# An mLSTM cell feeding a GELU feed-forward: the second chunk's cell moved into the first up projection, the first down projection with rows of w_out outermost, the first M spread by TensorE

## The chip, the cores and the metric

The kernel runs on one core of one Trainium2 chip. The metric is the device time of one execution in microseconds. The engines are named as in the profile: PE is TensorE's matmul, PEld its weight load, DVE is VectorE, ACT is ScalarE, POOL is GpSimd, SP is SyncE, whose queue issues nearly all transfers.

## The reference

An mLSTM cell over 4 batches, 8 heads, 768 steps and head size 40, then a feed-forward with exact GELU over the 3072 tokens that come out (320 values each, hidden size 2048):

```python
for t in range(S):
    m_new = np.maximum(f_gate[:, :, t] + m, i_gate[:, :, t])
    f_stab = np.exp(f_gate[:, :, t] + m - m_new)
    i_stab = np.exp(i_gate[:, :, t] - m_new)
    C = f_stab * C + i_stab * einsum('bhd,bhe->bhde', vt, kt)
    n = f_stab * n + i_stab * kt
    h_tilde = einsum('bhde,bhe->bhd', C, qt)
    denom = np.maximum(np.abs(einsum('bhd,bhd->bh', n, qt)), 1.0)
    y[:, :, t] = sigmoid(o_gate[:, :, t]) * h_tilde / denom
x = y.transpose(0, 2, 1, 3).reshape(B * S, H * D)
h = x @ w_in
out = (0.5 * h * (1.0 + erf(h / sqrt(2)))) @ w_out
```

The two weights come in as 64-bit floats; everything else is 32-bit.

## The kernel before, in words

**Chunks.** The 768 steps are cut into six chunks of 128. A chunk holds 4 batches of 128 tokens, 512 tokens in all. For each chunk a *cell* makes x (transposed, tile xT), an *up projection* makes g = gelu(x w_in) in eight steps, and a *down projection* makes the output from g and w_out. The order of a chunk is: up projection, then its down projection with the next chunk's cell woven in.

**The cell, per batch b (block n = 4c + b).** `turn` transposes k and q on PE and copies them out on ACT. The weights W[n] of the attention-like scores are exp(a_s - M_t), masked to s <= t: M, a running maximum per step, has to stand on all 128 partitions. Before, M is stored to a DRAM tile M_d and loaded back spread over the partitions (tile Mb, 512 KB a block, `load_M`); POOL masks it (`affine_select`), ACT takes the exps (L272, eight instructions with a bias of their own; for blocks 1 to 3 DVE subtracts first, L268, and one exp does, L269). `scores` multiplies q and k on PE (ps) and multiplies W into it on DVE (L317); it also forms the state update pc and the far part from the state (pf), with POOL scaling the values (vw) and the state. `values` multiplies W with v (ph), adds the far part (hs), and then gates and divides on POOL and DVE into a tile y. `turn_y` transposes y (px), and DVE and ACT copy the halves into xT.

**The weights.** w_in comes in 10 pieces and w_out in 16 (piece f is 128 rows of w_out). `fetch` loads raw bits into one of four buffers; `convert(i)` starts piece i and finishes piece i - 1: five DVE instructions and two ACT relus between them. The finish frees a buffer and issues fetch(i + 4). The first four up steps need pieces 0 to 4, the others 5 to 9.

**The up and down projections.** An up step takes two PSUM banks of the four-bank ring "mm" (which also holds the scores' banks and the down accumulators), 20 matmul records and two gelus on ACT. A down part is four rows of w_out for one batch; the four parts of batch 0 come first, so the first output needs all 16 rows. The accumulator goes out through o_sb.

**What sets the order.** Nothing is scheduled by the compiler: each engine works through its instructions in the program's order, and waits are semaphores between engines. SP's queue is in order too: a transfer that waits for a buffer holds those issued after it. `run_first` is the first cell with conversions 0 to 5; the rest of the conversions stand between the first up steps and inside the first four down parts; `run(fill)` is each later cell with 16 down parts placed in it by hand. The lookahead for q, k, v and o is six blocks (NLD); Mb has four buffers.

Of the kernel before, what the change touches and what calls it, by code (L numbers as in the profile page):

```python
# [16 lines left out]
I23 = 2.0 ** 23  # L17


@with_exitstack  # L20
def kernel(
# [72 lines left out]
    M_d = dram.tile([NCH, BH, L], F32, name="M_d")  # L94

    def load(n):

        if n >= NCH * B:
            return
        c, b = divmod(n, B)  # L100
        for src, dst in ((q, qb), (k, kb), (v, vb), (o_gate, ob)):
            nc.sync.dma_start(out=dst[n % NLD][:, :, 0:D],
                              in_=src[b, :, c * L:(c + 1) * L, :].rearrange("h p d -> p h d"))
# [3 lines left out]
    def load_M(n, eng=nc.sync):  # L107
# [5 lines left out]
        eng.dma_start(out=Mb[n].rearrange("p h l -> p (h l)"),  # L113
                      in_=M_d[c, b * H:(b + 1) * H, :].rearrange("h l -> (h l)").unsqueeze(0).to_broadcast([P, H * L]))
# [34 lines left out]
    for c0, c1 in ((0, 1), (1, NCH)):  # L149
# [92 lines left out]


    fetch(0)
    load(1)
    fetch(1)
    load(2)
    fetch(2)
    load(3)
    fetch(3)  # L250
    nc.sync.dma_start(out=M_d[1:NCH].rearrange("c p l -> p c l"), in_=M[:, 1:NCH])
# [7 lines left out]
    def weights_of(n):  # L259

        c, b = divmod(n, B)
        W[n] = wts.tile([P, H, L], F32, name="W", tag="W")
        M_n = Mb.pop(n)
        nc.gpsimd.affine_select(out=M_n, in_=M_n, compare_op=OP.is_ge, fill=1.0e30, base=0,  # L264
                                pattern=[[0, H], [1, L]], channel_multiplier=-1)
        if 0 < n < B:

            nc.vector.tensor_tensor(out=M_n, in0=M_n, in1=per_head(aT, c, b).to_broadcast([P, H, L]), op=OP.subtract)  # L268
            nc.scalar.activation(out=W[n], in_=M_n, func=AF.Exp, scale=-1.0)  # L269
        else:  # L270
            for h in range(H):
                nc.scalar.activation(out=W[n][:, h, :], in_=M_n[:, h, :], func=AF.Exp, scale=-1.0,  # L272
                                     bias=aT[:, c, b * H + h:b * H + h + 1])
        if c > 0:
            load_M(n + NM)

    def output_gate(n):
        nc.scalar.activation(out=ob[n % NLD], in_=ob[n % NLD], func=AF.Sigmoid)  # L278

    class Cell:  # L280


        def __init__(self, c):
            self.c = c
            self.qT, self.kT, self.far, self.ys = {}, {}, {}, {}
# [11 lines left out]
        def weighted(self, n):  # L297
            c, b = divmod(n, B)
            vw = two.tile([P, H, D1], F32, name="vw", tag="vw")
            nc.gpsimd.tensor_tensor(out=vw, in0=vb[n % NLD], in1=per_head(ewT, c, b).to_broadcast([P, H, D1]),  # L300
                                    op=OP.mult)
            return vw

        def scores(self, b, between=None):
            c, n = self.c, self.c * B + b
            kT, qT = self.kT.pop(b), self.qT.pop(b)
            if c + 1 < NCH and between is None:
                vw = self.weighted(n)
# [9 lines left out]
            if between is not None:  # L318
                between()
                vw = self.weighted(n)  # L320
# [3 lines left out]
            if c + 1 < NCH:  # L324
                for p in range(NP):
                    for hip in range(2):
                        nc.tensor.matmul(pc[halves[hip], p, :], kb[n % NLD][:, 2 * p + hip, :], vw[:, 2 * p + hip, :],  # L327
                                         start=True, stop=True)
# [19 lines left out]
        def values(self, b):  # L348
            c, n = self.c, self.c * B + b
# [5 lines left out]
            hs = two.tile([P, H, D1], F32, name="hs", tag="hs")  # L355
            if c > 0:
                nc.vector.tensor_tensor(out=hs, in0=ph, in1=self.far.pop(b), op=OP.add)
            else:
                nc.scalar.copy(out=hs, in_=ph)

            ys = self.ys[b] = two.tile([P, DM + R], F32, name="y", tag="y")
            y = ys[:, 0:DM].rearrange("p (h d) -> p h d", d=D)
            nc.gpsimd.tensor_tensor(out=y, in0=hs[:, :, 0:D], in1=ob[n % NLD], op=OP.mult)  # L363
# [7 lines left out]
            if c > 0:  # L371
                load(n + NLD)

        def turn_y(self, b):

            ys, t = self.ys.pop(b), slice(b * L, (b + 1) * L)
            for k0, n in ((0, 3), (3, 2)):
                px = ps_tr.tile([P, n, L], F32, name="px", tag="tr")
                for k in range(n):
                    nc.tensor.transpose(px[:, k, :], ys[:, (k0 + k) * R:(k0 + k + 2) * R], ident)  # L380
                nc.vector.tensor_copy(out=xT[0:R, k0:k0 + n, t], in_=px[0:R])  # L381
                nc.scalar.copy(out=xT[R:P, k0:k0 + n, t], in_=px[R:P])  # L382

        def run_first(self):

            self.turn(0), weights_of(0), convert(0)
            self.scores(0, decays)
            for b in range(1, B):
                weights_of(b)
            for b in range(B):  # L390
                if b > 0:
                    self.turn(b), convert(b)
                    if b == B - 1:
                        load(B)
                    self.scores(b), self.turn_y(b - 1)
                output_gate(b), self.values(b)
            load(B + 1)
            self.turn_y(B - 1), convert(B), convert(B + 1)

        def run(self, fill):  # L400

            n = self.c * B
            self.turn(0), weights_of(n), fill(2)
            self.turn(1), weights_of(n + 1), weights_of(n + 2), fill(1)
            self.scores(0), fill(1)
            self.turn(2), weights_of(n + 3)
            for b in range(B):
                output_gate(n + b)
            fill(1)
            self.scores(1), self.values(0), fill(2)  # L410
            self.turn(3), fill(1)
            self.scores(2), self.values(1), fill(1)
            self.turn_y(0), fill(1)
            self.scores(3), self.values(2), fill(1)
            self.turn_y(1), fill(1)
            self.values(3), fill(1)
            self.turn_y(2), fill(2)
            self.turn_y(3), fill(1)
# [18 lines left out]
    def down_steps(c, g):  # L437
        hold = {}

        def part(b, f0, f1):  # L440
# [5 lines left out]
            if f1 == NF:  # L446
                o_sb = outp.tile([P, DM], F32, name="o_sb", tag="o_sb")
                nc.scalar.copy(out=o_sb, in_=po)  # L448
                nc.sync.dma_start(out=out[b * S + c * L:b * S + (c + 1) * L, :], in_=o_sb)

        return [lambda b=b, f=f: part(b, f, f + 4) for b in range(B) for f in range(0, NF, 4)]

    def feeder(steps):
        todo = list(steps)

        def fill(n):
            for _ in range(min(n, len(todo))):
                todo.pop(0)()
        return fill

    Cell(0).run_first()
    gate_ctx.close()
    gp = ctx.enter_context(tc.tile_pool(name="gp", bufs=1))
    done = [n_in // 2 + 1]

    def conv(n):
        for _ in range(n):
            if done[0] <= len(pieces):  # L470
                convert(done[0])
                done[0] += 1

    for c in range(NCH):
        g = gp.tile([P, NF, TG], F32, name="g", tag="g")
        ups, downs = up_steps(g), down_steps(c, g)
        if c == 0:

            conv(1)
            for j, step in enumerate(ups):  # L480
                step()
                conv(1 if j == 2 else 2)
                if j in (2, 5):
                    load(B + 2 + j // 3)
                if j >= NF // 2 - B:
                    load_M(B + j - (NF // 2 - B))
            for i in range(1, 4):
                at, old = n_in + 4 * (i + 1), downs[i]
                downs[i] = lambda at=at, old=old: (conv(at + 1 - done[0]), old())
            downs[4] = lambda old=downs[4]: (load(2 * B), load(2 * B + 1), old())  # L490
        else:
            for step in ups:
                step()
        fill = feeder(downs)
        if c + 1 < NCH:
            Cell(c + 1).run(fill)
        fill(B * NF)
# [30 lines left out]
```

## Time and profile before

| | |
|---|---|
| median of 3 runs | 597.93 us (597.92 to 598.04) |
| the profiled execution | 598.42 us, span 596.6 us |
| PE busy | 552.7 us (93% of the span) |
| DVE, ACT, POOL busy | 205.2, 227.1, 81.1 us |
| mean granted TensorE clock | 0.977 |
| moved by DMA | 43.62 MB |

The page gives busy time by engine, the span in 40 slices, the DMA queues, the chain that ended last, and groups of instructions by line. A row of the timeline has start, duration, engine, line, operation, tiles, count, and in brackets the idle time before it with what ended it. A row of the windows has the stretch, its length, busy time of PE, PEld, DVE, ACT and POOL with their instruction counts, the granted clock, the share of DMA, and GB/s. A matmul on 32-bit floats shows as two records.

### The profile page before, as it was taken

The numbers are of one execution on the slowest core, as the hardware profiler recorded it, in microseconds if no ns is written. First come the engines' busy times: TensorE is split into PE (matmuls) and PEld (weight loads), VectorE is DVE, ScalarE is ACT, GpSimd is POOL, SyncE is SP. The second block draws the span as 40 slices with busy tenths as digits, with TensorE's granted clock in tenths as the row PEclk, the third lists the DMA queues.
The fourth block names the chain that finished last, engine by engine and source line by source line (L and its number), as shares of the span: only waits on it lengthen the run. The fifth ranks groups of instructions, "written<-read, shape, count | busy, mean of one in ns | idle before, by whom it ended". The sixth has DMA issues, their size and how long they took to land.

```text
span 596.6 us, 9412 instructions
## 1 busy us (share of the span) xinstructions
PE 552.7 (93%) x3850; PEld 355.7 (60%) x3850; DVE 205.2 (34%) x447; ACT 227.1 (38%) x496; POOL 81.1 (14%) x130
## 2 busy tenths in 40 slices
PE   2585999469999999999999999999999999999997
PEld 2474555347754577754577754577754577744575
DVE  6487888545610025610025600035600033500000
ACT  2654666752122382122481132481132581132100
POOL 3321000303210013310022300022400000100000
PEclk9998899769999999999999999999999999999999
DMA  9977878629820036510046600036000000000000
GB/s 193 203 125 118 164 162 217 226 73 162 137 36 1 0 121 123 88 33 1 1 138 115 96 17 0 1 150 104 13 12 0 1 12 12 12 12 0 1 22 22
DMA packets 111017, 43.62 MB, mean 73 GB/s; under 512 B 101248, under 2 KB 104512, under 8 KB 110976
## 3 DMA queue, kind: packets, MB, share of 16 engines
q1 hardware_dynamic: 110352, 40.92, 33.8%
q10 hardware_dynamic: 624, 2.11, 1.0%
q8 instruction: 30, 0.49, 0.4%
q14 instruction: 11, 0.09, 0.0%
HBM read 38.99 MB, written 4.03 MB: 72 GB/s over the span
## 4 chain that ended last, share of the span: by engine, by line
PE 79%; DVE 10%; issue 4%; DMA 4%; POOL 2%; ACT 1%; SPq 0%; DVEq 0%; POOLq 0%; ACTq 0%
PE po L445 34%; PE pu L430 29%; PE ps L314 3%; PE ph L354 3%; PE pt L292 3%; PE px L380 2%; PE pf L332 2%; DVE sig L232 2%; DMA bits<-in_moe_w_out_dram 2%; PE pf L327 1%; DVE pow L237 1%; DVE pow L225 1%; DMA bits<-in_moe_w_in_dram 1%; DMA Mb<-M_d 1%; DVE sig L230 1%
## 5 line engine op out<-in xcount | busy, mean ns | idle before, releaser
L445 PE MATMUL po<-w_out,g 128*128 128x320 f32 x768 | 224.3, 441 | 7.3 <-DVE w_out L239 7.3
L430 PE MATMUL pu<-xT,w_in 64*128 64x512 f32 x960 | 212.0, 597 | 0.4 <-DVE xT L381 0.2
L445 PEld LDWEIGHTS po<-w_out,g 128*128 128x128 f32 x768 | 142.0, 192 | 62.2 <-DVE w_out L239 9.9
L430 PEld LDWEIGHTS pu<-xT,w_in 64*128 64x128 f32 x960 | 97.8, 189 | 112.1 <-issue 109.2
L317 DVE TENSOR_TENSOR W<-ps,W 128x512 f32<-128x512 f32 x48 | 30.9, 685 | 256.4 <-PE ps L314 251.1
L433 ACT ACTIVATE g<-pu 128x512 f32<-128x512 f32 x96 | 52.0, 593 | 125.8 <-PE pu L430 125.8
L382 ACT COPY xT<-px 64x384 f32<-64x384 f32 (+1 forms) x48 | 17.9, 420 | 115.6 <-DVE xT L381 115.6
L272 ACT ACTIVATE W<-Mb,aT 128x128 f32<-128x128 f32 x168 | 50.8, 392 | 2.6 <-POOL Mb L264 2.5
L345 POOL TENSOR_TENSOR state<-state,dec 64x164 f32<-64x164 f32 x32 | 14.8, 461 | 232.6 <-PE pf L332 231.4
L314 PE MATMUL ps<-qT,kT 64*128 64x128 f32 x384 | 30.6, 304 | 8.2 <-ACT qT L295 8.2
L363 POOL TENSOR_TENSOR y<-hs,ob 128x320 f32<-128x320 f32 x24 | 19.4, 807 | 137.1 <-ACT ob L278 57.5
L314 PEld LDWEIGHTS ps<-qT,kT 64*128 64x128 f32 x384 | 25.7, 204 | 18.4 <-ACT qT L295 9.6
L264 POOL TENSOR_SCALAR_AFFINE_SELECT Mb<-Mb 128x1024 f32<-128x1024 f32 x24 | 28.1, 1192 | 60.3 <-DMA Mb<-M_d 60.0
L448 ACT COPY o_sb<-po 128x320 f32<-128x320 f32 x24 | 10.2, 426 | 58.3 <-PE po L445 42.8
L354 PE MATMUL ph<-vb,W 128*64 128x41 f32 x768 | 28.4, 235 | 2.6 <-DVE W L317 2.6
L354 PEld LDWEIGHTS ph<-vb,W 128*64 128x64 f32 x768 | 26.3, 145 | 5.9 <-DVE W L317 3.7
L381 DVE COPY xT<-px 64x384 f32<-64x384 f32 (+1 forms) x48 | 21.0, 475 | 16.7 <-PE px L380 16.4
L227 ACT ACTIVATE pow<-pow,e_hi 128x320 f32<-128x320 uint32 (+1 forms) x26 | 16.2, 622 | 23.9 <-DVE pow L225 23.8
L292 PE MATMUL pt<-ident,kb 128*128 128x128 f32 x96 | 17.3, 309 | 6.0 <-ACT kT L295 6.0
L295 ACT COPY kT<-pt 128x512 f32<-128x512 f32 x24 | 14.0, 585 | 23.0 <-PE pt L292 22.9
L380 PE MATMUL px<-ident,y 128*128 128x128 f32 x120 | 18.7, 291 | 3.0 <-DVE y L369 3.0
L292 PEld LDWEIGHTS pt<-ident,kb 128*128 128x128 f32 x96 | 12.8, 157 | 13.8 <-ACT kT L295 6.5
(74 smaller groups left out, 360.2 us busy)
## 6 DMA issues: line engine op xcount, KB each, us to landing
Mb<-M_d SPq DMA_DIRECT2D x20, 512.0 KB, 4.1
bits<-in_moe_w_in_dram SPq DMA_DIRECT2D x20, 256.0 KB, 5.0
bits<-in_moe_w_out_dram SPq DMA_DIRECT2D x16, 320.0 KB, 3.2
qb<-in_q_dram SPq DMA_DIRECT2D x24, 160.0 KB, 4.7
kb<-in_k_dram SPq DMA_DIRECT2D x24, 160.0 KB, 4.8
vb<-in_v_dram SPq DMA_DIRECT2D x24, 160.0 KB, 5.0
ob<-in_o_gate_dram SPq DMA_DIRECT2D x24, 160.0 KB, 4.3
out_dram<-o_sb SPq DMA_DIRECT2D x24, 160.0 KB, 1.8
```

What stands on the lines that cost most here:

```text
L264: nc.gpsimd.affine_select(out=M_n, in_=M_n, compare_op=OP.is_ge, fill=1.0e30, base=0, pattern=[[0, H], [1, L]], channel_multiplier=-1)
L272: nc.scalar.activation(out=W[n][:, h, :], in_=M_n[:, h, :], func=AF.Exp, scale=-1.0, bias=aT[:, c, b * H + h:b * H + h + 1])
L292: nc.tensor.transpose(pt[:, p, :], src[n % NLD][:, 2 * p:2 * p + 2, :].rearrange("p h d -> p (h d)"), ident)
L314: nc.tensor.matmul(ps[hip][:, p, :], kT[r, p, :], qT[r, p, :], start=True, stop=True)
L317: nc.vector.tensor_tensor(out=w, in0=ps[hip], in1=w, op=OP.mult)
L354: nc.tensor.matmul(ph[r, h, :], Pm[:, h, r], vb[n % NLD][:, h, :], start=True, stop=True)
L363: nc.gpsimd.tensor_tensor(out=y, in0=hs[:, :, 0:D], in1=ob[n % NLD], op=OP.mult)
L380: nc.tensor.transpose(px[:, k, :], ys[:, (k0 + k) * R:(k0 + k + 2) * R], ident)
L381: nc.vector.tensor_copy(out=xT[0:R, k0:k0 + n, t], in_=px[0:R])
L430: nc.tensor.matmul(pu[e], w_in[r, blk, i * P:(i + 1) * P], xT[r, (blk - e) % NK, :], start=(blk == 0), stop=(blk == NK - 1))
L433: nc.scalar.activation(out=g[:, f + e * (WP // P), :], in_=pu[e], func=AF.Gelu)
L445: nc.tensor.matmul(po, g[:, f, b * L:(b + 1) * L], w_out[:, f, :], start=(f == 0), stop=(f == NF - 1))
```

## The change

Four things are edited together.

1. The order of the steps is written as text. Each word is one step: T turn, M mask, W weights, S scores, C carry (the state part of the old `scores`), V values, Y finish (gate and divide), X turn_y, G gate, U an up step, F a down part or row, K a conversion, P a first fetch, L a load of a block's q, k, v, o, B a load of Mb, D decays, R the store of M; the digit is the block.
2. The second chunk's cell stands in the first up projection (UP_0) and runs over into the first down (DOWN_0).
3. The first down takes row f of w_out for all four batches at once, in four accumulators.
4. For chunk 0, M is spread over the partitions by PE: a column of the identity, repeated, as stationary operand, times M. ACT reads the result in PSUM, and the mask is laid on W after the exp. M_d and Mb are left for the later chunks.

Besides, y is written in place into the o tile, now 384 wide, so a block's load for six blocks on stands behind X in place of V; and px of chunk 0 takes the ring mm.

```diff
+FIRST = """
+    W0 T0 P W1 W2 D L1 P K M0 P P T1 S0 V0 M1 L2 R C0 K S1 G0 V1 M2 K G1 T2 Y0 K G2 X0 W3 L3 K S2 L4 C1 B4 V2 Y1 X1
+    T3 G3 M3 Y2 B5 S3 L5 C2 B7 V3 K C3 Y3 B6 X2 X3"""
+UP_0 = """
+    M0 T0 K G0 U L6 W0 S0 M1 C0 W1 M2 T1 M3 U K K U S1 V0 W2 L8 C1 U K W3 T2 K U K L7 Y0 K U U K K U T3 G1 V1 L9 S2
+    G2 S3 K C2 V2 K Y1 F F Y2 X0 F K F F K K X1 F K C3"""
+DOWN_0 = """
+    V3 K F K F X2 F F F F G3 K K K F F Y3 K F X3 F"""
+DOWN = """
+    M0 T0 W0 F F M1 M2 T1 W1 W2 F S0 C0 F M3 T2 W3 G0 G1 G2 G3 F S1 C1 V0 Y0 F F T3 F S2 C2 V1 Y1 F
+    X0 F S3 C3 V2 Y2 F X1 F V3 Y3 F X2 F F X3 F"""
...
-    ob = [const.tile([P, H, D], F32, name=f"ob{n}") for n in range(NLD)]
+    ob = [const.tile([P, DM + R], F32, name=f"ob{n}") for n in range(NLD)]
...
-        if c0 == 0:
-            nc.scalar.dma_start(out=M_d[0], in_=M[:, 0])
-            for n in range(B):
-                load_M(n, nc.scalar)
...
+        def mask(self, b):
+            t, fill = (Mb[self.c * B + b], 1.0e30) if self.c > 0 else (W[b], 0.0)
+            nc.gpsimd.affine_select(out=t, in_=t, compare_op=OP.is_ge, fill=fill, base=0,
+                                    pattern=[[0, H], [1, L]], channel_multiplier=-1)
+
+        def weights(self, b):
+            n = self.c * B + b
+            W[n] = wts.tile([P, H, L], F32, name="W", tag="W")
+            if self.c > 0:
+                M_n = Mb.pop(n)
+            for h in range(H):
+                r = b * H + h
+                if self.c > 0:
+                    src = M_n[:, h, :]
+                else:
+                    if h % 4 == 0:
+                        pm = ps_mm.tile([P, 4, L], F32, name="pm", tag="mm")
+                        for j in range(4):
+                            nc.tensor.matmul(pm[:, j, :], ident[0:BH, r + j:r + j + 1].to_broadcast([BH, P]), M[:, 0, :],
+                                             start=True, stop=True)
+                    src = pm[:, h % 4, :]
+                nc.scalar.activation(out=W[n][:, h, :], in_=src, func=AF.Exp, scale=-1.0, bias=aT[:, self.c, r:r + 1])
+            if self.c > 0:
+                load_M(n + NM)
...
+        def row(f):
+            if f == 0:
+                hold["po"] = [ps_mm.tile([P, DM], F32, name="po", tag="mm") for b in range(B)]
+            for b in range(B):
+                nc.tensor.matmul(hold["po"][b], g[:, f, b * L:(b + 1) * L], w_out[:, f, :],
+                                 start=(f == 0), stop=(f == NF - 1))
+                if f == NF - 1:
+                    send(b, hold["po"][b])
...
+    for c in range(-1, NCH):
         if c == 0:
...
+        steps = dict(K=conv, P=first_fetch, L=load, R=store_M, B=load_M, D=decays)
         if c + 1 < NCH:
+            cell = Cell(c + 1)
+            steps |= dict(M=cell.mask, W=cell.weights, G=cell.gate, T=cell.turn, S=cell.scores, C=cell.carry,
+                          V=cell.values, Y=cell.finish, X=cell.turn_y)
+        if c >= 0:
+            g = gp.tile([P, NF, TG], F32, name="g", tag="g")
+            steps |= dict(U=in_turn(up_steps(g)), F=in_turn(down_steps(c, g)))
+            play(UP_0 if c == 0 else "U " * (NF // 2), **steps)
+        play(FIRST if c < 0 else "F " * (B * NF // 4) if c + 1 == NCH else DOWN_0 if c == 0 else DOWN, **steps)
```

More of the change, by code (lines that the diff above doesn't have):

```diff
@@ L295, in turn, with scores @@
                 nc.scalar.copy(out=store[b], in_=pt)
[L297 to L308, printed above, removed]
+        def scores(self, b):
+            n = self.c * B + b
+            kT, qT = self.kT.pop(b), self.qT[b]
             ps = [ps_mm.tile([P, NP, L], F32, name="ps", tag="mm") for hip in range(2)]
@@ L324, in scores @@
             if c + 1 < NCH:
+                vw = two.tile([P, H, D1], F32, name="vw", tag="vw")
+                nc.gpsimd.tensor_tensor(out=vw, in0=vb[n % NLD], in1=per_head(ewT, c, b).to_broadcast([P, H, D1]),
+                                        op=OP.mult)
                 for p in range(NP):
@@ L384, in run_first @@
[L384 to L398, printed above, removed]
@@ L454, in feeder, with in_turn @@
+    def in_turn(steps):
         todo = list(steps)
[L456 to L476, printed above, removed]
-        if c == 0:
[L479 to L494, printed above, removed]
-        if c + 1 < NCH:
-            Cell(c + 1).run(fill)
-        fill(B * NF)
```

128 lines of the change are left out of this document (56 added, 72 removed).

## The prediction

> **What bounds the kernel now.** I read the page first, then busy time by stage, then the stretches in which PE idles.
>
> ```profile
> span 596.6 us, 9412 instructions
> PE 552.7 (93%) x3850; PEld 355.7 (60%) x3850; DVE 205.2 (34%) x447; ACT 227.1 (38%) x496; POOL 81.1 (14%) x130
> ```
>
> PE is the bound over the whole span; the question is where its other 44 us lie. Windows at the stage borders (first column the stretch, then its length, busy time and instructions of each engine, granted clock, DMA share, GB/s):
>
> ```profile
> 0.00:58.70 58.70, 31.73 (x326) 26.52 (x326) 39.78 (x83) 27.56 (x54) 16.20 (x42) 0.97 0.86 159
> 58.70:97.70 39.00, 38.82 (x160) 20.79 (x160) 34.06 (x74) 26.66 (x46) 1.34 (x1) 0.92 0.83 178
> 97.70:170.80 73.10, 59.80 (x501) 43.92 (x500) 41.83 (x92) 31.30 (x75) 17.39 (x23) 0.88 0.73 146
> 170.80:205.30 34.50, 34.50 (x161) 15.41 (x160) 0.00 (x0) 9.31 (x16) 0.00 (x0) 1.00 0.02 5
> 205.30:259.50 54.20, 54.20 (x502) 41.28 (x500) 23.44 (x52) 23.07 (x59) 14.19 (x20) 1.00 0.48 98
> 160.00:596.00 436.00, 433.15 (x2938) 272.35 (x2936) 94.80 (x210) 143.51 (x327) 51.03 (x69) 1.00 0.18 40
> ```
>
> In order: cell of chunk 0; first up projection; first down projection with cell 1 inside; then the same two stages one chunk later, undisturbed. From 160 us on PE is busy 433.15 of 436 us, so nothing is to be won there. The first up takes 39.0 against 34.5 us, the first down 73.1 against 54.2, for the same instructions: 4.5 + 18.9 = 23.4 us are lost. The first cell's 58.7 us is a latency chain with PE half idle. These 82 us hold everything the edit can move. PE in the first down (start, duration, in brackets the idle before it and its releaser):
>
> ```profile
> 109.17 1.12 PE L292 MATMUL pt<-ident,kb 128*128 128x128 f32 x4 [6.03 <-ACT kT L295]
> 121.27 1.43 PE L445 MATMUL po<-w_out,g 128*128 128x320 f32 x2 [4.72 <-DVE w_out L239]
> 123.32 1.44 PE L445 MATMUL po<-w_out,g 128*128 128x320 f32 x2 [0.62 <-DVE w_out L239]
> 126.69 2.50 PE L445 MATMUL po<-w_out,g 128*128 128x320 f32 x4 [1.93 <-DVE w_out L239]
> 140.24 0.60 PE L292 MATMUL pt<-ident,kb 128*128 128x128 f32 x4
> ```
>
> 6.03 + 4.72 + 0.62 + 1.93 = 13.3 us of plain idling. Behind each idle the clock is low: the same four transposes take 1.12 us at 109 and 0.60 at 140, which with slow matmuls makes up the other 5.6 us. The chain and SP's own timeline say why:
>
> ```profile
> 102.49 6.65 DMA Mb<-M_d
> 119.48 5.04 DMA bits<-in_moe_w_out_dram
> 109.03 10.37 SPq L113 DMA_DIRECT2D Mb<-M_d  x4
> ```
>
> A token block needs all 16 rows of w_out before its sum is complete, so the first block waits for the whole conversion, and the last raw rows ("bits") sit in SP's queue behind four Mb loads that wait for buffers for 10.37 us.
>
> **The change, part by part.** *Rows of w_out outermost in the first down.* The count of matmuls stays (16 rows x 4 blocks); row f is needed only when it is used, so a late row delays 2.2 us of work instead of a block. Alone it costs nothing: four accumulators take the four banks of the mm ring, which no score or up step needs by then; the four output copies fall together at the end, but the next up step needs only the first two banks.
>
> *Cell 1 inside the first up.* PE's work until the second up projection is that of the undisturbed pair, 34.5 + 54.2 = 88.7 us, less the first turn (0.9) that fits in the wait for the last xT copy: 87.8. DVE must fit in: one conversion of a w_in piece and one of a w_out piece, each a window around exactly one:
>
> ```profile
> 59.00:61.75 2.75, 2.75 (x7) 1.58 (x9) 2.65 (x6) 1.90 (x4) 0.00 (x0) 0.50 1.46 143
> 92.18:94.23 2.05, 2.05 (x13) 1.13 (x12) 1.95 (x6) 1.48 (x3) 0.00 (x0) 1.00 0.80 245
> ```
>
> After the first cell 21 K steps stay: 4 x 2.75 + one mixed 2.4 + 16 x 2.05 = 46.2, less 1.0 as the last only finishes; with cell 1's 23.44 DVE has 68.7 us of work under 87.8 of PE. DVE is no bound.
>
> ACT is tighter. In the up stretch before the last gelu (order text UP_0 up to the eighth U):
>
> ```profile
> 143.36 1.16 PE L314 MATMUL ps<-qT,kT 64*128 64x128 f32 x16
> 144.45 0.67 PE L327 MATMUL pf<-vw,kb 128*64 128x41 f32 x16
> 144.94 0.77 PE L332 MATMUL pf<-state,qT 128*64 128x82 f32 x16
> 145.54 1.08 PE L354 MATMUL ph<-vb,W 128*64 128x41 f32 x32
> L227 ACT ACTIVATE pow<-pow,e_hi 128x320 f32<-128x320 uint32 (+1 forms) x26 | 16.2, 622 | 23.9 <-DVE pow L225 23.8
> L295 ACT COPY kT<-pt 128x512 f32<-128x512 f32 x24 | 14.0, 585 | 23.0 <-PE pt L292 22.9
> L433 ACT ACTIVATE g<-pu 128x512 f32<-128x512 f32 x96 | 52.0, 593 | 125.8 <-PE pu L430 125.8
> 110.92 2.45 ACT L272 ACTIVATE W<-Mb,aT 128x128 f32<-128x128 f32 x8
> L272 ACT ACT_TABLE_LOAD x5 | 6.4, 1283 | 0.1
> 109.63:113.37 3.74, 3.74 (x14) 2.91 (x13) 2.80 (x4) 3.73 (x10) 1.60 (x2) 0.55 0.64 225
> ```
>
> Eight pairs of gelu at about 1.06 = 8.5; four blocks of eight exps at 2.45 = 9.8; the relus of nine K steps, two each at 0.62 = 11.2; six copies of turns at 0.585 = 3.5; a gate 0.5; and seven table loads at 1.28 = 9.0, since exp and gelu now alternate (gelu, exp, gelu, exp, gelu, exp, gelu; sigmoid is still loaded for the first gate). Sum 42.5. PE in that stretch: 34.5 + two more turns 1.8 (each two sets of four transposes at 0.60, less their overlap) + two scores 2.3 + two carries 2.6 (0.67 + 0.77, less overlap) + one values 1.0 = 42.2. So ACT is level with PE, and what decides is when each gelu frees its banks. Walking the order with these durations, from the first U at 0: gelu 1 ends at 5.4; the exps of blocks 0 and 1 at 11.5; gelu 2 at 15; gelu 3 at 19, when PE is just ready for U4; gelu 4 at 25. Before gelu 5 stand relus, a table load and the exps of block 3, copies, relus and another load: it ends at 34.9, while PE wants its banks for U7 at 33.1. One stall, **1.8 us**; bounds 0 (the copies run ahead) and 8 x 3.74 = 29.9 (a load and eight exps ahead of every gelu).
>
> That window (a table load and eight exps, 3.74 us, ACT busy 3.73) also bears on a rule. The Trainium skill, page "ScalarE: Activation LUTs", section "What ACT_TABLE_LOAD costs", puts a switch at 1283 ns plus a drain of about 1380 ns, and its section "Table sets: the hidden batching unit" says to do all calls of one set before switching, which speaks against this order. The load agrees with the row; a drain doesn't show in it. By that page the seven switches would cost 7 x 1.38 = 9.7 us more, and the time would be 586.7.
>
> *Clock at the start of the up.* The first cell still leaves PE sparse, so the first up starts slow again: 39.0 x (1 - 0.92) = **3.1 us**. Bounds 0 (PE dense from the new matmuls) and 4.5 (the whole loss of that stage).
>
> *Bits for the last rows.* Four buffers, so a fetch goes out when the piece four earlier is done. The last one goes out at the second K of DOWN_0, some 76 us after the first U; a landing takes 3.2 us (median) to 5.04, with a load of q, k, v and o beside it, and its K is due 4 to 5 us later: **1.0 us**, bounds 0 and 5.04.
>
> ```profile
> bits<-in_moe_w_out_dram SPq DMA_DIRECT2D x16, 320.0 KB, 3.2
> 0.00:125.00 125.00, 86.25 (x578) 57.84 (x578) 92.02 (x195) 72.81 (x145) 23.45 (x50) 0.91 0.82 175
> Mb<-M_d ACTq DMA_DIRECT2D x4, 512.0 KB, 8.1
> ```
>
> By volume it holds: 125 us at 175 GB/s is 21.9 MB; the four 512 KB Mb loads of chunk 0 go (-2.1), two blocks of loads (+1.3) and one Mb (+0.5) move ahead of the last bits: 21.6 MB, 123 us, with the last piece due near 140. The Mb loads still hold SP until exps are done, but each set of exps is done by 31 us after the first U, and the bits queued behind have 4 to 14 us to spare.
>
> *First M by TensorE, and the first cell's order.* This removes the M_d store, the four loads, the subtractions on DVE and one-instruction exps; it adds 32 matmuls (32 rows, 128 columns) and cuts three one-instruction blocks of exps into eight each, on ACT, which isn't the chain there.
>
> ```profile
> 7.43 1.11 PE L292 MATMUL pt<-ident,kb 128*128 128x128 f32 x4
> 11.74 1.11 PE L292 MATMUL pt<-ident,qb 128*128 128x128 f32 x4 [3.20 <-DVE aT L177]
> 13.76 2.08 PE L314 MATMUL ps<-qT,kT 64*128 64x128 f32 x16 [0.90 <-ACT qT L295]
> 21.20 0.33 DVE L188 COPY dec<-pd 128x160 f32<-128x160 f32 x1 [1.05 <-PE pd L186]
> 21.81 5.25 DVE L268 TENSOR_TENSOR Mb<-Mb,aT 128x1024 f32<-128x1024 f32 x3 [0.29 <-POOL Mb L264]
> 30.42 0.17 DVE L365 SCALAR_TENSOR_TENSOR den<-hs 128x8 f32<-128x8 f32 x1 [3.36 <-ACT hs L359]
> 40.79:49.13 8.34, 6.63 (x16) 1.00 0.24 66
> 47.09 0.17 DVE L365 SCALAR_TENSOR_TENSOR den<-hs 128x8 f32<-128x8 f32 x1 [1.43 <-ACT hs L359]
> 58.73 2.07 PE L430 MATMUL pu<-xT,w_in 64*128 64x512 f32 x3 [0.22 <-DVE xT L381]
> ```
>
> A matmul of f32 shows as two records. One block of M is 16: between 2.08 (the scores, two row halves at once) and 16 x 1.11/4 = 4.4 (turns). I take 3.3, between them as the shape is a turn's and the count a score's. Two blocks and the decays follow the first turn, which ends at 11.74 + 1.11 = 12.9 as it waits for aT. The decays are ten small transposes at about half a turn's 0.28 (1.4), a matmul and copies of 0.33 partly beside them: about 2.2. So dec is there at 12.9 + 6.6 + 2.2 = 21.7; I take 21.5, as now; bounds 12.9 + 4.2 + 2.2 = 19.3 and 12.9 + 8.8 + 2.2 = 23.9. From there DVE is the chain. One block's round now, from K step to K step, holds a K, a scores multiply, an xT copy and a finish; it takes 8.34 us, of which 1.43 are the wait for hs: 6.91 of work. Four of these, half a K (1.4) and one K more (2.75) make 31.8. The new order puts a K or another block's copies into the waits; I leave 3 us of them (first scores 1.5; last values, finish and xT 1.5): the first U at 21.5 + 31.8 + 3 = **56.3** against 58.73. Bounds: no wait and an early dec, 51.1; 3.36 + 4 x 1.43 = 9.1 us of waits and a late dec, 64.8.
>
> *The order text DOWN for the later chunks* is the old run's order with the same places for F; Y writes into ob in place of y, and loads come after X rather than after V, over a chunk before they are read: 0. Bounds: the 2.85 us that PE idles from 160 on, both ways.
>
> **Sum.** Second up at 56.3 + 87.8 + 1.8 + 3.1 + 1.0 = 150.0 against 170.8: -20.8. The profiled execution took 598.42 us, 1.8 more than its span; 598.42 - 20.8 = 577.6. The median of runs shown (597.93) is 0.5 below that execution: **577 us**.
>
> **Rivals.**
> 1. *SP's queue starves the conversions.* The Mb loads in UP_0 hold SP as at 109 us, so the w_out waits of now (7.3 us) or those with the 6.03 return: 584 to 590. For: fetches still share SP's queue with Mb and loads. Against: rows are used one at a time.
> 2. *A switch costs ACT more than its load*, say its length again: seven times 1.28 on the engine that is level with PE, 577 + 9.0 = 586. Against: ACT is busy 3.73 of the 3.74 us around a load. (The page named above has such a cost, the drain.)
> 3. *PE finds all it needs*: waits in the first cell shrink, the up starts warm, no gelu stall: 577 - 3 - 3.1 - 1.8 - 1.0 = 568, up to 572 with half.
> 4. *Slower: the four-bank ring locks.* Every U waits until its ring predecessor's gelu, itself behind a load and eight exps. 3.74 us at each of eight U: 577 + 29.9 - 1.8 = 605. It decides from 21 + 1.8 = 22.7 us, 2.8 per U. For: ACT and PE are level and the ring holds two U's. Against: only four blocks of exps stand among eight U's, and U3, U6, U8 have none ahead.
> 5. *The edit doesn't do what it says*: rows are late however ordered, and the first cell doesn't shorten: 595 to 600.
>
> **How the numbers follow.** My case (572 to 582) 0.52; rival 1 0.17; 2 0.05; 3 0.16; 4 0.06; 5 0.04. Below 569 lie some 0.07, above 590 some 0.12: range 569 to 590. A difference under 0.2% is what a measurement of this kernel can't tell from none. Faster 0.90 (all but 4 and most of 5), same 0.03, slower 0.07.
>
> **What would show it.** The first pu near 56, the 160th pu record near 103 among cell 1's lines, the second up near 150; 54.2 and 34.5 us for later stages; no DVE w_out idle over 1 us before po; about eight table loads on ACT between 57 and 110. I am wrong if PE idles in the first up for ACT g, if SP waits for ACT W while DVE waits for bits, or if the first pu comes after 60.

## The result, and the profile after

The changed kernel takes **579.94 us** (median of 4 runs, 577.55 to 581.53) against 597.92 (596.51 to 598.04) of the kernel before in the same comparison: a ratio of 0.9701, 95% interval 0.9665 to 0.9738. The forecast was 577 us, range 569 to 590. The profiled execution took 579.88 us. The page:

```profile
span 578.2 us, 9535 instructions
PE 558.8 (97%) x3914; PEld 365.5 (63%) x3914; DVE 200.8 (35%) x444; ACT 238.8 (41%) x524; POOL 82.1 (14%) x130
```

PE has 64 records more than before (those of M) and is busy for 6 us more, in a span that is 18.4 us shorter. Windows at the new stage borders, with the same columns as before. The rows are the first cell; the first up and first down projection with the second cell in them; the second up; the second down. "First U" is the first matmul of the first up projection, "second up" that of the second chunk's, and "the stage" the time between them.

```profile
0.00:61.90 61.90, 47.22 (x398) 42.29 (x399) 41.22 (x90) 35.62 (x82) 17.86 (x44) 1.00 0.89 149
61.90:152.40 90.50, 89.25 (x652) 58.69 (x652) 69.38 (x155) 61.16 (x120) 18.12 (x23) 1.00 0.82 166
152.40:186.90 34.50, 34.50 (x161) 15.41 (x160) 0.00 (x0) 9.73 (x17) 0.00 (x0) 1.00 0.06 20
186.90:241.10 54.20, 54.20 (x502) 41.28 (x500) 23.62 (x52) 23.07 (x59) 14.18 (x20) 1.00 0.51 97
```

The whole gain lies in the second row, the stage. It took 170.8 - 58.7 = 112.1 us before and takes 90.5 now, with PE busy in all but 1.25 us of it. The first row went the other way: the first cell takes 61.9 us where it took 58.7. The later stages are the 34.5 and 54.2 us of before. So -21.6 + 3.2 = -18.4 us of span.

Two questions were left: which part of the edit carries the gain, and why the first cell became longer when it should have become shorter. PE in the first cell (start, duration, line, operation, tiles, shape, count, in brackets the idle before it and its releaser):

```profile
7.51 3.76 PE L307 MATMUL pm<-M,ident 32*128 32x128 f32 x16
13.10 7.19 PE L307 MATMUL pm<-M,ident 32*128 32x128 f32 x32
24.32 2.08 PE L336 MATMUL ps<-qT,kT 64*128 64x128 f32 x16
52.71 1.16 PE L336 MATMUL ps<-qT,kT 64*128 64x128 f32 x16 [0.68 <-ACT qT L326]
61.92 0.66 PE L425 MATMUL pu<-xT,w_in 64*128 64x512 f32 x1
```

The same scores (ps) take 2.08 us at 24 and 1.16 at 53: PE runs at about half its rate for the first 50 us. In the windows of the same stretch the clock column doesn't say so (sixth item after the length: 1.00), and PE isn't idle either while M is spread:

```profile
11.20:22.70 11.50, 10.99 (x55) 10.49 (x55) 1.33 (x4) 8.56 (x28) 3.67 (x4) 1.00 1.22 201
22.70:61.90 39.20, 31.70 (x324) 27.59 (x324) 31.52 (x65) 25.27 (x52) 9.21 (x11) 1.00 0.78 134
```

In the second of these rows DVE is busy for 31.52 of 39.2 us. Its timeline there says what it lacked (dec, the decay factors, is where DVE's chain of work begins):

```profile
22.72 0.33 DVE L204 COPY dec<-pd 128x160 f32<-128x160 f32 x1 [1.05 <-PE pd L202]
26.50 1.29 DVE L339 TENSOR_TENSOR W<-ps,W 128x512 f32<-128x512 f32 x2 [2.06 <-PE ps L336]
32.53 1.29 DVE L339 TENSOR_TENSOR W<-ps,W 128x512 f32<-128x512 f32 x2 [2.02 <-PE ps L336]
```

The view of its waits in the same stretch (us in total, times, the longest) adds them up; four waits for scores are 5.5 us:

```profile
DVE W L339 <- PE ps L336: 5.5, 4, 2.1
```

The kernel before, from its dec to its first U:

```profile
21.50:58.70 37.20, 24.05 (x282) 20.47 (x278) 27.32 (x53) 19.99 (x38) 8.65 (x10) 0.95 0.83 130
```

So dec now ends 1.5 us later (23.05 against 21.53), DVE has 3.9 us more work between it and the first U (31.2 against 27.3: two and a half more conversions, and no subtractions), and DVE waits 2.2 us less (7.7 against 9.9). Part of the longer first cell is thus conversion work that the stage no longer has to do.

### The profile page after: what moved, and what is told of

It reads as the page before. It is cut to its first block, busy times and chain, and to the rows that moved or that the text cites. A ratio compares the mean times of both kernels' runs of the same rounds, so it can differ in the third digit from the quotient of the medians.

```text
span 578.2 us, 9535 instructions
## 1 busy us (share of the span) xinstructions
PE 558.8 (97%) x3914; PEld 365.5 (63%) x3914; DVE 200.8 (35%) x444; ACT 238.8 (41%) x524; POOL 82.1 (14%) x130
## 4 chain that ended last, share of the span: by engine, by line
PE 90%; DVE 6%; ACT 2%; issue 1%; DMA 0%; SPq 0%; DVEq 0%; ACTq 0%
PE pu L425 35%; PE po L455 31%; PE ps L336 5%; PE ph L381 4%; PE pt L323 4%; PE po L440 3%; PE pm L307 2%; PE px L409 2%; PE pf L359 2%; PE pf L354 2%; DVE sig L248 1%; DVE pow L253 1%; DVE W L339 1%; DVE w_out L255 1%; DVE sig L246 0%
## 5 line engine op out<-in xcount | busy, mean ns | idle before, releaser
L425 PE MATMUL pu<-xT,w_in 64*128 64x512 f32 x960 | 209.9, 591 | 0.5 <-ACT g L428 0.4
L455 PE MATMUL po<-w_out,g 128*128 128x320 f32 x640 | 183.2, 436 | 0.0
L425 PEld LDWEIGHTS pu<-xT,w_in 64*128 64x128 f32 x960 | 94.5, 187 | 111.2 <-issue 106.9
L411 ACT COPY xT<-px 64x384 f32<-64x384 f32 (+1 forms) x48 | 17.9, 420 | 101.4 <-DVE xT L410 101.4
L310 ACT ACTIVATE W<-Mb,aT 128x128 f32<-128x128 f32 x160 | 48.4, 392 | 0.1
L391 POOL TENSOR_TENSOR ob<-hs,ob 128x320 f32<-128x320 f32 x24 | 19.9, 829 | 135.9 <-ACT ob L316 70.5
L440 PE MATMUL po<-w_out,g 128*128 128x320 f32 x128 | 35.9, 435 | 0.8 <-DVE w_out L255 0.8
L381 PE MATMUL ph<-vb,W 128*64 128x41 f32 x768 | 29.7, 239 | 2.6 <-DVE W L339 1.5
L289 POOL TENSOR_SCALAR_AFFINE_SELECT Mb<-Mb 128x1024 f32<-128x1024 f32 x20 | 22.7, 1160 | 2.9 <-DMA Mb<-M_d 2.7
L409 PE MATMUL px<-ident,ob 128*128 128x128 f32 x120 | 18.6, 287 | 4.1 <-DVE ob L397 3.8
```

The lines of the kernel that those rows point to most:

```text
L289: nc.gpsimd.affine_select(out=t, in_=t, compare_op=OP.is_ge, fill=fill, base=0, pattern=[[0, H], [1, L]], channel_multiplier=-1)
L310: nc.scalar.activation(out=W[n][:, h, :], in_=src, func=AF.Exp, scale=-1.0, bias=aT[:, self.c, r:r + 1])
L381: nc.tensor.matmul(ph[r, h, :], Pm[:, h, r], vb[n % NLD][:, h, :], start=True, stop=True)
L409: nc.tensor.transpose(px[:, k, :], ob[n % NLD][:, (k0 + k) * R:(k0 + k + 2) * R], ident)
L425: nc.tensor.matmul(pu[e], w_in[r, blk, i * P:(i + 1) * P], xT[r, (blk - e) % NK, :], start=(blk == 0), stop=(blk == NK - 1))
L440: nc.tensor.matmul(hold["po"][b], g[:, f, b * L:(b + 1) * L], w_out[:, f, :], start=(f == 0), stop=(f == NF - 1))
```

## The experiments

All are edits of the changed kernel, and each was timed against the kernel before on the same chip. That kernel's median was 595.86 us beside e1 to e4, 596.10 beside e6 to e9 and 596.36 beside e10 to e12, so the ratios compare better than the medians. First U, second up and stage are those of the one execution that was traced: it was the fastest of its runs in e8 (574.82 us) and the slowest in e2 (583.13) and e12 (576.41). The numbers first, the reasons below:

| kernel | median us (range) | ratio, 95% interval | first U | second up | stage |
|---|---|---|---|---|---|
| before | 597.92 | 1 | 58.73 | 170.82 | 112.1 |
| changed | 579.94 (577.55 to 581.53) | 0.9701 [0.9665, 0.9738] | 61.92 | 152.43 | 90.5 |
| e4_cell_in_down | 594.00 (591.74 to 596.62) | 0.9965 [0.9943, 0.9987] | 59.47 | 164.46 | 105.0 |
| e6_blocks_first | 603.85 (600.60 to 605.35) | 1.0115 [1.0068, 1.0163] | 62.29 | 176.82 | 114.5 |
| e7_more_switches | 592.61 (591.48 to 594.66) | 0.9945 [0.9923, 0.9967] | 60.08 | 165.07 | 105.0 |
| e1_m_by_dma | 575.39 (574.34 to 575.95) | 0.9641 [0.9619, 0.9664] | 58.24 | 148.24 | 90.0 |
| e3_rows128 | 577.97 (577.77 to 578.23) | 0.9686 [0.9662, 0.9710] | 59.55 | 150.65 | 91.1 |
| e8_rows128_early | 576.86 (574.82 to 578.70) | 0.9669 [0.9625, 0.9714] | 56.80 | 147.33 | 90.5 |
| e9_dma_filler | 573.94 (573.85 to 575.26) | 0.9629 [0.9586, 0.9671] | 56.12 | 146.63 | 90.5 |
| e12_dma_turn_first | 574.21 (571.71 to 576.41) | 0.9636 [0.9591, 0.9681] | 58.25 | 149.22 | 91.0 |
| e2_decays_early | 580.76 (579.12 to 583.13) | 0.9736 [0.9703, 0.9770] | 64.87 | 155.68 | 90.8 |
| e10_early_m2_late | 580.23 (579.80 to 581.98) | 0.9748 [0.9714, 0.9783] | 61.41 | 152.36 | 91.0 |
| e11_early_rows128 | 580.52 (578.80 to 581.86) | 0.9742 [0.9709, 0.9775] | 61.51 | 152.55 | 91.0 |

### The stage: which part of the edit carries it

**The cell goes back into the first down, by blocks of tokens; the new first cell stays.**

```diff
 # UP_0: K's and loads among the U's only
+    K U K K U K K U K L6 U K K U K K U K K L7 U K K U K K
 ...
 # DOWN_0: the order of the later chunks with K's
+    M0 T0 W0 F F M1 M2 T1 W1 W2 K F S0 C0 K K K K F M3 T2 W3 G0 ...
...
-        if c == 0:
-            return [lambda f=f: row(f) for f in range(NF)]
```

> The changed kernel with chunk 1's cell back in the first down projection and that projection by token blocks, conversions placed as before; the new first cell, M by TensorE and in-place y stay. (Rows outermost cannot stay: its four accumulators hold the ring that the scores need.) Theory A, the gain is that of the move: first up matmul at 62, the stage up plus down 110-114 us again, second up at 172-176, total 599-604. Rival, the gain comes from the smaller DMA load (M no longer moved): second up at 155-165, total 582-593.

594.0 us, between the two; the second up, at 164.46, lies in the rival's range. PE's timeline in the first down:

```profile
114.27 1.44 PE L455 MATMUL po<-w_out,g 128*128 128x320 f32 x2 [6.39 <-DVE w_out L255]
116.32 1.44 PE L455 MATMUL po<-w_out,g 128*128 128x320 f32 x2 [0.61 <-DVE w_out L255]
119.91 2.50 PE L455 MATMUL po<-w_out,g 128*128 128x320 f32 x4 [2.15 <-DVE w_out L255]
```

The waits for w_out of the kernel before are back, 9.2 us of them. Move and rows together carry 594.0 - 579.9 = 14 of the 18 us by the medians, and about 16 by the ratios. The stage of 105.0 is still 7 us shorter than before (2.5 us of it in the up, 4.6 in the down); the new order and the absence of chunk 0's Mb loads, which the rival named, share these 7 us, and no run splits them. Beside the move and the rows these loads cost the stage nothing: e1 below has them again, and its stage is 90.0.

**The cell stays in the up, and the first down goes by blocks of tokens.** (The fourth combination, rows with the cell in the down, was not tried: the four accumulators take the ring that the scores of the cell need.)

```diff
-        if c == 0:
-            return [lambda f=f: row(f) for f in range(NF)]
...
 # DOWN_0, end of UP_0: the K's ahead of the F's that need them
-    V3 K F K F X2 F F F F G3 K K K F F Y3 K F X3 F
+    V3 K K F X2 K K K K F F F F G3 F F F F Y3 F X3 F F F F
```

> The changed kernel with cell 1 still in the first up projection, but the first down by token blocks (four rows of w_out for one batch, batch 0 first) in place of rows outermost; K steps moved ahead of the parts that need them, the first F's thinned out to match. Theory A, rows outermost carry their own share: the first block can't end before the last conversion, near 138-142, and 13 parts of 2.25 us follow: second up at 163-170 in place of 152, total 591-598. Theory B, the move of the cell alone brings the gain, the conversions are done in time anyhow: second up at 152-156, total 580-584.

Worse than either theory: 603.85 us, 1.2% slower than the kernel before, with an interval clear of 1. The view of waits:

```profile
PE po L455 <- DVE w_out L255: 12.9, 8, 3.7
```

and two of these waits in PE's timeline:

```profile
119.50 0.81 PE L455 MATMUL po<-w_out,g 128*128 128x320 f32 x2 [3.67 <-DVE w_out L255]
143.13 1.44 PE L455 MATMUL po<-w_out,g 128*128 128x320 f32 x2 [2.47 <-DVE w_out L255]
```

So the move needs the rows; whether the rows need the move is not tested. The move alone, in this order of the K's, puts the cell's DVE work ahead of the conversions and makes the first down wait longer for them (12.9 us in eight waits, and slow matmuls behind each). With rows outermost the conversions are needed one at a time.

**Eleven more table switches**, to see whether ACT is level with PE in the up stretch and what a switch costs.

```diff
+            if extra:
+                nc.scalar.activation(out=scr, in_=e_hi, func=AF.Sigmoid, scale=0.0)
```

> The changed kernel with one sigmoid of a 128x1 tile (result unused) after the two gelus of each up step of the first chunk: eight tiny instructions and some 11 more table loads of 1.28 us, 14 us of work on ScalarE in the first up. Theory A, ScalarE is level with TensorE there (38.94 of 41.1 us busy): the stage from the first up matmul to the second up grows from 90.5 by 9-14 us, total 589-594. Theory B, it has slack: growth under 3 us, total 580-583. If a switch also drains, as the Trainium skill has it, growth of 20 us or more.

A sigmoid of 128x1 stands behind the gelus of each U of the first chunk, and the next gelu or exp must load its table again: 23 loads instead of 12 up to the second up, 11 x 1.28 = 14.1 us, and eight sigmoids of 0.20 us. The groups of instructions between 60 and 165 us (count, busy us and mean ns, idle before):

```profile
L430 ACT ACT_TABLE_LOAD x8 | 10.3, 1283 | 0.1
L432 ACT ACT_TABLE_LOAD x8 | 10.3, 1283 | 0.1
L310 ACT ACT_TABLE_LOAD x3 | 3.8, 1283 | 0.1
```

and the window of the up stretch:

```profile
60.00:117.00 57.00, 50.25 (x360) 29.12 (x360) 29.97 (x65) 56.17 (x98) 7.25 (x10) 0.97 0.70 155
```

The stage grew by 14.5 of the 15.7 us that were added, and ACT is busy for 56.17 of the 57 us: it has become the bound at once, so it was nearly level with PE. A switch costs its load and nothing else that shows; ACT's idle time in this window is 0.83 us in all. The Trainium skill, "ScalarE: Activation LUTs", section "What ACT_TABLE_LOAD costs", has a drain of some 1380 ns with each switch. An estimate from that figure makes eleven switches 29.3 us, and this run doesn't agree with it.

### The first cell: why it became longer

**M of chunk 0 goes through DRAM again, as in the kernel before; all the rest stays.**

```diff
+        if c0 == 0:
+            nc.scalar.dma_start(out=M_d[0], in_=M[:, 0])
+            for n in range(B):
+                load_M(n, nc.scalar)
...
-                if self.c > 0:
+                if True:
                     src = M_n[:, h, :]
```

> The changed kernel, with M of chunk 0 spread by a DRAM round trip as before in place of TensorE; the order text and the mask after the exps stay. Theory A, the first cell now waits for a PE at half rate and the 64 records of pm (14.9 us) stand on its path: the first up matmul moves from 61.9 to 53-56 us and the total falls to 571-575. Theory B, the order's own waits and the work of VectorE set the first cell and pm is beside it: first up matmul at 61-63, total 579-582.

The first U fell between the two, the time close to the faster one: without this part of the change the kernel is 4.5 us faster by the medians and 3.6 by the ratios, whose intervals only just lie apart. PE in e1:

```profile
58.24 4.59 PE L428 MATMUL pu<-xT,w_in 64*128 64x512 f32 x20
148.24 34.60 PE L428 MATMUL pu<-xT,w_in 64*128 64x512 f32 x160
```

The first U comes 3.7 us earlier, and the stage is the same. Spreading M on PE, in this form, is a net cost.

**Decays ahead of the weights of blocks 1 and 2**, so that dec doesn't queue behind their M.

```diff
-    W0 T0 P W1 W2 D L1 P K M0 P P T1 S0 V0 M1 L2 R C0 K S1 G0 V1 M2 K G1 ...
+    W0 T0 P D L1 P K M0 P P S0 W1 T1 V0 M1 L2 R C0 K S1 G0 W2 V1 M2 K G1 ...
```

> The changed kernel; in FIRST the decays and the first scores stand ahead of the M of blocks 1 and 2 (D before W1, S0 before W1, W2 after G0). Nothing is removed. Theory A (PE at half rate is the chain): VectorE starts its chain 6-7 us earlier, but PE's queue is as long as before: first up matmul at 57-60, total 575-578. Theory B (VectorE's chain from the decays on): the whole 6-7 us come through, first up matmul at 55-56, total 573-574. If neither: 62 and 580.

Both theories missed. The time is 580.76 us, as expected "if neither", and the first U of the traced execution, the slowest of four, comes at 64.87, the latest of all. dec is there at 17.9, 5 us earlier, and the time is lost again behind it. DVE waits 6.1 us for the second scores, which stand behind W1, T1, V0 and C0 on a slow PE. Then PE waits 4.75 us:

```profile
38.47 1.30 PE L409 MATMUL px<-ident,ob 128*128 128x128 f32 x5 [4.75 <-DVE ob L397]
64.87 2.08 PE L425 MATMUL pu<-xT,w_in 64*128 64x512 f32 x4
```

On POOL the mask of block 2 waits for the exps of the late W2 until 35.42, and the multiply of Y0, which PE needs, stands behind it. **With that mask behind Y0** and nothing else altered:

```diff
-    ... G0 W2 V1 M2 K G1 T2 Y0 K G2 ...
+    ... G0 W2 V1 K G1 T2 Y0 M2 K G2 ...
```

> The kernel with the decays and first scores early (first up matmul at 64.9, 580.8 in total), with one word moved: M2, POOL's mask of block 2, behind Y0. There the mask stood in POOL's queue ahead of Y0's multiply and waited for exps that the reordering had made late; VectorE waited 3 us for Y0 and TensorE 4.75, after which it ran at half rate. Theory A, this queue cost it: first up matmul at 57-60, total 574-577. Theory B, the late M of block 2 itself or the shorter queue on TensorE: 62-65 still, total 578-581.

The first U comes at 61.41 in a traced execution of 579.80 us (e2's took 583.13), and the median stays at 580.23. Half of the reason was right: DVE's wait behind the mask is gone, but the one for the second scores stands:

```profile
29.82 1.29 DVE L339 TENSOR_TENSOR W<-ps,W 128x512 f32<-128x512 f32 x2 [6.10 <-PE ps L336]
```

**M with 128 rows.** The records of M took 3.6 to 3.8 us a block, on a PE that was nearly always busy. Here M is copied into a tile with zeros in its other 96 rows, and the matmuls take all 128 rows; their count and columns stay.

```diff
+    nc.gpsimd.memset(Mx, 0.0)
...
+    nc.vector.tensor_copy(out=Mx[0:BH], in_=M[:, 0])
...
-    nc.tensor.matmul(pm[:, j, :], ident[0:BH, r + j:r + j + 1].to_broadcast([BH, P]), M[:, 0, :],
+    nc.tensor.matmul(pm[:, j, :], ident[:, r + j:r + j + 1].to_broadcast([P, P]), Mx,
```

> The changed kernel, with M of chunk 0 copied into a tile of 128 rows, zero below row 32, and the 32 matmuls of pm on 128 rows in place of 32: the same columns, the same count. Theory R, the rows in use count for whether PE leaves half rate: a block of pm falls from 3.76 us to about 2 from the second block on, first up matmul at 55-58, total 574-577. Theory N, they don't: pm stays at 3.6-3.8 a block, first up matmul at 61.5-62.5, total 579-581.

```profile
10.45 3.78 PE L310 MATMUL pm<-Mx,ident 128*128 128x128 f32 x16 [2.64 <-DVE Mx L183]
15.04 3.74 PE L310 MATMUL pm<-Mx,ident 128*128 128x128 f32 x32
```

The first block takes 3.78 us, the two after it 3.74 together, 1.87 each: PE leaves half rate by the end of the first block. With 32 rows it didn't within three blocks, though it was busy for 10.99 of 11.5 us; nor did it in e4, e6 and e7, which have the same first cell. The Trainium skill, "TensorE: Matmul & The Clock Gate", section "What's actually happening", lets the full clock come after some 3.4 us of sustained work; with 128 rows this trace agrees, with 32 rows it doesn't. A block over 32 rows isn't slow of itself, though. In e2 one stands behind work at full rate:

```profile
29.59 2.05 PE L307 MATMUL pm<-M,ident 32*128 32x128 f32 x16
```

In e3 the full rate doesn't last (the scores at 47.31 take 2.08 us again). Its first U, at 59.55, is no earlier than that of e4 (59.47), which spreads M over 32 rows, so the gain isn't shown by it. The copy stood behind all the scans and let PE wait 2.64 us. **With the copy right behind the first scan:**

```diff
+        if c0 == 0:
+            nc.vector.tensor_copy(out=Mx[0:BH], in_=M[:, 0])
```

> As the kernel with pm on 128 rows, with the copy of M into the 128-row tile right behind the first chunk's scan, so that pm can start near 7.7 in place of 10.45 us. If TensorE's queue in front of the first scores is the chain: decays 2 to 3 us earlier, first up matmul at 56.5-58, total 574.5-576.5. If the chain runs on VectorE's conversions and on POOL's order: first up matmul at 59-60 as there, total 577-579.

M starts at 9.04, and the first U comes at 56.80 instead of 61.92, in the fastest of four executions. The median is 576.86; its interval overlaps those of e3 and of the changed kernel. The trace shows the gain where it should lie, the times can't confirm it.

**M by DRAM, with three unused 128x128 by 128x328 matmuls behind T0 and again behind T2**, so that PE has full-height work in the two lean spots.

```diff
-    W0 T0 P W1 W2 D ... T2 Y0 K
+    W0 T0 Z P W1 W2 D ... T2 Z Y0 K
+    def fill():
+        pz = ps_h.tile([P, H, D1], F32, name="pz", tag="h")
+        for _ in range(3):
+            nc.tensor.matmul(pz..., ident, vb[0]..., start=True, stop=True)
```

> The kernel with M of chunk 0 by DMA, and three unused matmuls of 128x128 by 128x328 put into TensorE's idle time at two places of the first cell (behind the first turn, and behind the third). Theory A, the clock decides: the matmuls after each place run at full rate (scores 1.16 in place of 2.08 us), first up matmul at 55-57 in place of 58.2, total 572-574. Theory B, the chain is on VectorE and its waits: first up matmul at 58-59, total 575-577.

573.94 us, the lowest median of all; its interval [0.9586, 0.9671] overlaps e1's, so against e1 it is not settled. PE's timeline:

```profile
12.66 3.06 PE L277 MATMUL pz<-vb,ident 128*128 128x328 f32 x6
25.45 1.16 PE L345 MATMUL ps<-qT,kT 64*128 64x128 f32 x16
56.12 4.81 PE L434 MATMUL pu<-xT,w_in 64*128 64x512 f32 x19
```

and a window of the first cell:

```profile
20.00:56.00 36.00, 24.82 (x311) 20.60 (x309) 32.92 (x64) 27.62 (x59) 12.28 (x13) 0.83 1.07 192
```

The scores take 1.16 us from 25 on (PE is back at half rate for a while: the values at 41.16 take 1.73 us, at 28.06 1.02), and DVE is busy for 32.92 of 36.0 us: 3.1 us of waits, with the first U at 56.12.

Two more tried to join the pieces. **e8's M in e10's order:**

> The same order as the run with M2 behind Y0, with pm on 128 rows and an early copy of M. If the clock and POOL's queue are the two things that hold the first cell: first up matmul at 54-56, total 571-574. If VectorE's own work is what is left (31.5 us from the decays on): 56-57, total 574-577, no better than the 576.9 of 128 rows alone.

Both theories missed: 580.52 us and a first U at 61.51, a higher median than e8 has in the order of the change, with intervals that overlap a little. In its trace DVE waits 3.84 us for the second scores, and PE 4.71 us for a copy of xT at 41.86; what delays that copy was not followed. **e9 with the first turn ahead of all weights** (T0 D Z P W0 W1 W2 ... S0 T1):

> The kernel with M by DMA and the unused matmuls (573.9), with the first turn and the decays ahead of the exps of block 0, and the first scores ahead of the second turn: the copies of the turn no longer wait on ScalarE for M's landing. If VectorE's idle time before the first scores (11.9 to 18.7 us) is what is left: decays near 16 in place of 20.6, first up matmul at 52-54, total 569.5-572. If the landing of M (near 15) and its exps set the chain: 55-56, total 573-575.

In the traced execution, the slowest of four, dec is there at 16, and the first U still comes at 58.25. From the timelines of DVE and PE:

```profile
23.12 0.43 DVE L245 TENSOR_SCALAR pow<-bits 128x512 uint32<-128x512 uint32 x1 [1.31 <-DMA bits<-in_moe_w_in_dram]
29.34 1.11 PE L332 MATMUL pt<-ident,kb 128*128 128x128 f32 x4 [0.43 <-DMA kb<-in_k_dram]
```

DVE and PE now wait for the DMAs themselves, and PE is back at half rate. An early dec was worth nothing in this execution. Two of the other three took 571.71 and 572.38 us, close to what was expected if DVE's early idle time were what is left. No trace shows them, so this stays open.

## Why the prediction was right, and where it was not

**The stage** was forecast at 150.0 - 56.3 = 93.7 us, 18.4 less than before, and took 90.5, 21.6 less. That the move and the rows fill it was right, and e4 and e6 bear it out. Two windows and two rows of PE's timeline:

```profile
60.00:66.00 6.00, 5.51 (x30) 3.96 (x29) 5.54 (x10) 4.86 (x10) 2.57 (x3) 1.00 0.85 178
61.90:103.00 41.10, 40.68 (x293) 23.49 (x295) 28.54 (x60) 38.94 (x78) 7.74 (x11) 1.00 0.94 207
```

```profile
96.76 9.34 PE L425 MATMUL pu<-xT,w_in 64*128 64x512 f32 x40 [0.40 <-ACT g L428]
145.23 4.57 PE L440 MATMUL po<-w_out,g 128*128 128x320 f32 x16 [0.83 <-DVE w_out L255]
```

Term by term:

- *PE's work*, 87.8: 89.25 was measured. The 160 records of the up steps (L425) are busy for 36.85 us here and for 34.60 in the next chunk, those of the down for 35.81 and 36.97, so the other 1.45 us lie in the up steps; no run says why.
- *The gelu stall*, 1.8: 0.40, once, where it was forecast (ACT g, the seventh U). That ACT is level with PE was right: 38.94 us busy of 41.1, four loads of gelu's table, three of exp's and one of sigmoid's between 57 and 112 us. e7 shows what happens when that margin is used up.
- *The clock at the start of the up*, 3.1: nothing in this execution. The clock column shows 1.00 from 60 to 66 us (before, 0.50 from 59.00 to 61.75), and the last rows of the cell are fast already. The last blocks of the cell had brought PE to full rate at 51 us. This is half of rival 3.
- *Bits for the last rows*, 1.0: the size was right (0.83) and the cause wrong. It is a wait for a conversion that DVE ran slowly, beside POOL's masks of the next chunk (below), and not for a DMA.

**The first U** was forecast at 56.3, in bounds of 51.1 to 64.8, and came at 61.92, past the 60 that the prediction had named as a sign of being wrong. This is the step that failed, in two terms:

- *dec*, 21.5: 23.05. The two blocks of M took 7.2 us instead of 6.6, the decays 2.8 instead of 2.2. I had set M between the scores and the turns of a PE at half rate, and half rate is what came; the sizes were off. I had not asked whether so much work would bring PE to full rate, which would have made both shorter. With 128 rows it does (e3), with 32 it didn't.
- *Waits of DVE*, 3: 7.7, while DVE's work itself came as forecast (31.2 after dec against 31.8). The 3 us took the new order's cover as given, while PE at half rate makes each set of scores 0.9 us later. Four traces of this same first cell bear it out. Where the second scores take 2.08 us, the waits are 7.7 us (the changed kernel) and 7.8 (e6) and the first U comes at 61.92 and 62.29; where they take 1.16, the waits are 5.1 us (e4) and 5.8 (e7) and the first U comes at 59.47 and 60.08. With M off PE the waits are 3.5 us in e1 and 3.1 in e9, where the first U comes at 56.12. So the term holds for a PE without M, which this change doesn't have.

That the sum came out within 0.5% is luck, because the errors have opposite signs: +5.6 for the first U, and in the stage -3.1 for the clock, -1.4 for the stall, -0.2 for the bits, +1.45 for PE's work. Together +2.4, which is the second up at 152.43 against 150.0, and most of the 2.9 us by which the median misses.

**The rivals.** SP's queue didn't starve the conversions, the ring didn't lock, and a switch cost only its load. Rival 5 was right in part: the first cell doesn't shorten, it becomes longer.

**What stays open.** Why PE's change of rate falls at another moment in each execution: at 51 us in the changed kernel, between 24 and 29 in e4 and e7, which have the same first cell, at 25 in e1, and back again behind waits of a few us. A difference of 2 us in the first U of two single traces therefore shows little. And whether the first cell can go below 56 us: by e9's window DVE is then the bound, and no run took work from DVE.

## What to carry to other kernels

A stage with PE nearly full can take in another stage's latency chain, but ask in which order it needs its late inputs: the move paid with the loop turned so that the converted rows are needed one at a time, and without that, in the order tried, it made the kernel 1.2% slower. Don't price work on an engine at its rate elsewhere; look whether the same shape takes the same time before and after, and whether the new work is of the kind that brings the rate up. And cost every part of a combined change by itself: here one part (M on PE) cost about 4 us inside a gain of 18.

## What the runs showed of the hardware

- Three blocks of matmuls over 32 rows left PE at half rate (3.76 us, then 7.19 for two), in the changed kernel, e4, e6 and e7 alike, while the same matmuls over 128 rows ran at 1.87 us from the second block on (e3, e8). Behind work at full rate a block over 32 rows took 2.05 us (e2). The clock column of the changed kernel shows 1.00 for both rates in its first 60 us; the durations of equal shapes are the better witness.
- DVE's conversions take two to four times as long beside POOL's masks. DVE's and POOL's timelines:

```profile
137.67 0.31 DVE L241 TENSOR_SCALAR pow<-bits 128x320 uint32<-128x320 uint32 x1
140.19 1.09 DVE L241 TENSOR_SCALAR pow<-bits 128x320 uint32<-128x320 uint32 x1
...
139.76 3.60 POOL L289 TENSOR_SCALAR_AFFINE_SELECT Mb<-Mb 128x1024 f32<-128x1024 f32 x3
```

The same instruction takes 0.31 us ahead of the three masks and 1.09 beside them. The Trainium skill, "GPSIMD Engine Reference", section "1. Specifications", says that the two engines share their SBUF interfaces, with contention for DVE instructions in a 2-port mode or with two SBUF inputs. These rows agree with a contention; which of the two cases holds isn't shown, and no run took the masks away.
